# Sparse attention and token mix: scores two units ahead, exponentials in front of evictions, edge queries loaded sooner

## The chip, the cores and the metric

The kernel runs on one core of a Trainium2 chip. The metric is the device time of one execution in microseconds. The core has five engines that each work through their own queue in order: TensorE (PE: matmuls, and their weight loads PEld), VectorE (DVE), ScalarE (ACT), GpSimd (POOL) and SyncE (SP, which here only issues DMA transfers). They wait for each other by semaphores.

## The reference

Block-sparse attention over 4 batches, 8 heads, 768 positions and a head size of 64, in blocks of 32 positions (24 blocks), followed by a token mix. An inner block of queries sees its neighbours, the first and last block of keys, and three sampled blocks; the first and last block of queries see all keys.

```
scores = scale * np.matmul(q, k.transpose(0, 1, 3, 2))
mask = np.abs(blk_i - blk_j) <= window
mask = mask | (blk_i == 0) | (blk_j == 0) | (blk_i == n_blocks - 1) | (blk_j == n_blocks - 1)
...
scores = np.where(mask, scores, -1000000000.0)
attn = softmax(scores)
x = attn @ v                       # heads put side by side, d_model 512
theta = x @ w_theta
y = w_tok_r @ (x * cos(theta)) + w_tok_i @ (x * sin(theta))   # over the 768 positions
u = x + y
out = u + maximum(u @ w_ch, 0)
```

All is in float32, and the four weights of the mix come as 64-bit words that the kernel decodes into a high and a low part.

## The kernel before

The attention is cut into 56 **units**, worked on by a software pipeline that `attention` writes out by hand: under `tc.manual_schedule()` each engine runs its instructions in the order in which the Python code issues them. The units of the first two batches (bp = 0) are six edge units, named w (the first and last block of queries against a third of all keys, twice three of them), and 22 inner units (query blocks 1 to 22); then the same for the other two batches (bp = 1). `half` is 28. A unit's stages, each a function called as `do(n, stage)`:

- `scores` (L332, L340): 32 matmuls on PE (16 for an edge unit) into one of two PSUM places S, and on DVE one reduction that gives m (L343).
- `weights` (L360): four exponentials on ACT, from S and m into P.
- `turn` (L370): eight transpositions of P on PE into two PSUM banks T.
- `evict` (L376): two copies on ACT from T into pT.
- `values` (L394): matmuls of pT with the values (va, vb) on PE into X.
- `finish` (L401 to L403): the normalisation on DVE, or for an edge unit a copy (L417).

Around these run the preparations, called as `inner(n, ...)` for inner units alone. Keys of a unit are copied side by side into one of two buffers `kgs`: the window and two sampled blocks on POOL (`gather_window` L298, `gather_keys` L277), the third sampled block on ACT (`gather_key` L280). Values come by a gathering DMA that POOL issues (`gather_values` L314) and by a window load on SP, with a copy on POOL in front of it (`load_window` L310, L307). Queries come by `load_q` on SP (L242), two units at a time, and ACT scales them (`scale_q` L247). Edge queries come by `load_edges` (L258) and are scaled by `scale_edges`. `join` puts edge units together on POOL during later steps (L431). `store` writes results to a buffer in memory (L422).

Between the stages, a `Decoder` turns the weights into two parts, in shares that are due by step: ACT starts a piece (L63) and rounds its high part (L81), DVE does the rest (L68 to L86), and the raw words are loaded through ACT's queue (L59).

One step n of the loop before, as each engine sees it:

| engine | its instructions in order |
| --- | --- |
| PE | scores(n+1), turn(n), values(n-1) |
| DVE | reduction of n+1, up to two decoder shares, finish(n-1) |
| ACT | decoder start, evict(n), weights(n+1), gather_key(n+3), scale_q(n+3), decoder's high part |
| POOL | gather_window(n+3), gather_keys(n+3), gather_values(n+2), window copy of n+1, one piece of a join |
| SP | load_q(n+6), window load of n+1, store(n-1), key loads for bp = 1, edge queries at n = 24 |

After the loop comes the token mix, whose first parts `next(follow)` mixes into the last six steps. Its pools take the memory of the attention, so its bulk begins when the last unit is done. The listing has the functions around the change.

Of the kernel before, what the change touches and what calls it, by code (L numbers as in the profile page):

```python
# [10 lines left out]
F32 = mybir.dt.float32  # L11
# [8 lines left out]
P = 128  # L20
# [163 lines left out]
def attention(tc, qT, qE, kT, vr, sampled, xs, ident, early_pieces, late_pieces, first_place, follow, spares):  # L184
# [14 lines left out]
    with ExitStack() as ctx, ExitStack() as early:  # L199
# [10 lines left out]
        wp = ctx.enter_context(tc.tile_pool(name="wp", bufs=2))  # L210
# [9 lines left out]
        def make_places(bp):  # L220

            if bp == 0:
                place = first_place([P, 13824], F32, "kv0")
                k = place[:, 0:6144]
                wide[bp] = [place[:, 6144 + 1040 * c : 6144 + 1040 * (c + 1)] for c in range(6)]
            else:
                k = kp.tile([P, 6144], F32, name="k1")
                wide[bp] = vbs + vbs[:2]
            ks[bp] = k.rearrange("r (s g f) -> r s g f", s=NB, g=8)

        def load_k(bp, s0, n, queue=nc.sync):
            queue.dma_start(ks[bp][:, s0 : s0 + n].rearrange("r s g f -> r s (g f)"), kT[bp][:, s0 : s0 + n])

        def load_wide(bp, t, queue=nc.sync):
            for c in (2 * t, 2 * t + 1):
                queue.dma_start(wide[bp][c], vr[768 * bp + 128 * c : 768 * bp + 128 * c + 128])
# [16 lines left out]
        def scale_edges(bp):  # L253
            scale(qes[bp].rearrange("r b p f -> r (b p f)"))

        def load_edges(bp):
            qes[bp] = ep.tile([P, 2, 4, 64], F32, tag="qe", name=f"qe{bp}")
            nc.sync.dma_start(qes[bp].rearrange("r b p f -> r (b p f)"), qE[bp])  # L258
# [62 lines left out]
        def scores(unit):  # L321

            bp, i, x = unit
            s = st[unit] = {}
            sc = ps_s[units.index(unit) % 2].tile([P, 2, 2, 256], F32, tag="S", name=f"S{name(unit)}")
            heads = [(b, p, e) for b in range(2) for p in range(4) for e in range(2)]
            if i == "w":
                t, a = x
                q, keys = qes[bp], ks[bp][:, 8 * t : 8 * t + 8]
                for b, s_, e in [(b, p, e) for b, p, e in heads if p < 2]:  # L330
                    rows, p = slice(64 * e, 64 * e + 64), 2 * a + s_
                    nc.tensor.matmul(sc[64 * s_ : 64 * s_ + 64, e, b, :], q[rows, b, p, :], keys[rows, :, 4 * b + p, :], start=True, stop=True)  # L332
                if t == 0:
                    mxs[a] = wp.tile([P, 3, 4], F32, tag="mx", name=f"mx{name(unit)}")
                m = mxs[a][:, t]
            else:
                q, keys = qbs.pop((bp, i)), kgs[i % 2]
                for b, p, e in heads:
                    rows = slice(64 * e, 64 * e + 64)
                    nc.tensor.matmul(sc[32 * p : 32 * p + 32, e, b, :], q[rows, b, p, :], keys[rows, :, 4 * b + p, :], start=True, stop=True)  # L340
                m = wp.tile([P, 4], F32, tag="m", name=f"m{name(unit)}", bufs=2)

            nc.vector.tensor_reduce(m.rearrange("r (e b) -> r e b", e=2), sc, axis=AX.X, op=ALU.min)  # L343
            if i == "w" and t == 2:

                top = wp.tile([P, 4], F32, tag="top", name=f"top{name(unit)}", bufs=1)
                nc.vector.tensor_tensor(top, mxs[a][:, 0], mxs[a][:, 1], op=ALU.min)
                nc.vector.tensor_tensor(top, top, m, op=ALU.min)
                fs[a] = wp.tile([P, 3, 4], F32, tag="fs", name=f"fs{name(unit)}")
                nc.vector.tensor_tensor(fs[a], mxs[a], top.unsqueeze(1).to_broadcast([P, 3, 4]), op=ALU.subtract)  # L350
            s["S"] = sc, m
# [90 lines left out]
        units = []  # L442
        for bp in range(NP):
            units += [(bp, "w", (t, a)) for t in range(3) for a in range(2)] + [(bp, i, None) for i in range(1, NB - 1)]
        half = len(units) // 2

        def name(unit):
            bp, i, x = unit
            return f"{bp}_w{x[0]}{x[1]}" if i == "w" else f"{bp}_{i}"

        def do(n, stage, *args):
            if 0 <= n < len(units):
                stage(units[n], *args)

        def inner(n, stage):
            if 0 <= n < len(units) and units[n][1] != "w":
                stage(*units[n][:2])

        spares.append(lambda: qp.tile([P, 4, 4, 32], F32, tag="q", name=f"spare{len(spares)}", bufs=Q_BUFS))
        with tc.manual_schedule():
            load_edges(0)
            make_places(0)
            load_k(0, 0, 8)
            tab = Tables(nc, cp, sampled)

            nc.vector.memset(first, 0.0)
            nc.scalar.activation(first, first, AF.Exp)  # L470
            idle = ps_x.tile([P, P], F32, tag="X", name="idle")
            for _ in range(WARM):
                nc.tensor.matmul(idle, ident, ident, start=True, stop=True)
            decoder = Decoder(early_pieces + late_pieces, stage, nc.scalar)
            load_wide(0, 0)
            load_k(0, 8, 8)
            load_wide(0, 1)
            load_k(0, 16, 8)
            decoder.load(0, nc.sync)
            load_q(0, 1)  # L480
            load_wide(0, 2)
            decoder.load(1, nc.sync)
            load_q(0, 3)
            make_places(1)
            scale_edges(0)
            do(0, scores)
            making = tab.make(nc, cp)
            next(making)
            do(0, weights)
            steps = len(units) + 1  # L490
            for n in range(steps):
                if n == len(units) - 1:
                    early_s.close()
                    next(follow)

                if n <= half:
                    due = 3 * len(early_pieces) * max(n - 3, 0) // (half - 3)
                else:

                    weight = lambda k: 4 * min(k, 6) + 7 * max(k - 6, 0)  # L500
                    due = 3 * len(early_pieces) + 3 * len(late_pieces) * weight(n - half) // weight(len(units) - 4 - half)
                due = min(due, 3 * len(decoder.pieces)) - decoder.at
                decoder.first_on_scalar(due)
                do(n + 1, scores)
                next(making, None)
                inner(n + 4, number_blocks)
                inner(n + 3, gather_window)
                inner(n + 3, gather_keys)
                if due > 0:
                    decoder.on_vector()  # L510
                if due > 1 and decoder.at % 3:
                    decoder.on_vector()
                do(n, turn)
                do(n - 1, values)
                if len(units) - 2 <= n < len(units):
                    next(follow)
                do(n, evict)
                do(n + 1, weights)
                inner(n + 3, gather_key)
                inner(n + 3, scale_q)  # L520
                decoder.on_scalar()
                do(n - 1, finish)
                if units[min(n + 6, steps - 2)][:2] not in ((0, 1), (0, 3)):
                    inner(n + 6, load_q)
                inner(n + 2, gather_values)

                inner(n + 1, lambda bp, i: load_window(bp, i) if i > 2 else None)
                inner(n + 3, lambda bp, i: load_window(bp, i) if i <= 2 else None)
                inner(n - 1, store)

                if n <= len(units) and units[n - 1][1:] in (("w", (2, 0)), ("w", (2, 1))):
                    joins.append(join(units[n - 1][0], units[n - 1][2][1]))
                if n % half > 6 and joins and next(joins[0], joins) is joins:
                    joins.pop(0)
                if 5 <= n < 29 and n % 2:
                    load_k(1, n - 5, 2)
                if n == 24:
                    load_edges(1)
                if n == half - 3:
                    scale_edges(1)  # L540
                for t, step in enumerate((half - 2, half, half + 2)):
                    if n == step:
                        load_wide(1, t)

                if n == len(units) - 4:
                    early.close()
                if len(units) - 6 <= n < len(units):
                    next(follow)
            assert not decoder.left() and not joins, (decoder.left(), joins)
# [395 lines left out]
```

## Time and profile before

| what | us |
| --- | --- |
| median of three runs | 596.28 |
| lowest and highest of them | 595.65 and 603.92 |
| the profiled execution, its own time | 599.4 |
| span of its instructions | 597.6 |
| first and last reduction of an inner unit (L343) start at | 29.7 and 249.5 |

The profile shows one execution, and its times count from the first instruction. "Busy" is the time in which an engine executes an instruction. A wait is put down to the instruction whose end released it; "issue" is time in which an engine waited for nothing that the profile shows. Ends of matmuls are modelled. The granted clock is the share of full speed at which TensorE was allowed to run.

### The profile page before, as it was taken

Reading aid. Unit: us, or ns where it says so; the run is one execution under the profiler, and the core shown is the slowest. Engines: PE = TensorE matmul, PEld = TensorE weight load, DVE = VectorE, ACT = ScalarE, POOL = GpSimd, SP = SyncE. Lnnn points to the kernel's source line nnn. Section 1 sums busy time; section 2 is a strip of 40 time slices with the busy share of each in tenths; the row PEclk is TensorE's granted clock in tenths of the full one; section 3 lists DMA queues with packets and bytes.
Section 4 is the critical chain, followed back from the end, with each engine's and each line's share of the span. In section 5 each row is a group of like instructions: output and inputs, shape, how many; then the busy total and the mean of one; then the engine's idle time right before and its main releaser. Section 6 shows DMA issues by size and latency. Waiting matters only on the chain.

```text
span 597.6 us, 17323 instructions
## 1 busy us (share of the span) xinstructions
PE 548.1 (92%) x7092; PEld 436.6 (73%) x7092; DVE 423.8 (71%) x846; ACT 335.6 (56%) x684; POOL 180.8 (30%) x281
## 2 busy tenths in 40 slices
PE   6997886979967878999999999999999999999997
PEld 4765555556645545678888888888888888888886
DVE  3786876977889999968999996557732759613352
ACT  4797876758978866875565653344630445521220
POOL 1387957942687888530010010000000000000000
PEclk9898988979999998899999999999999999999999
DMA  8979889879988996852333132220212311102002
GB/s 313 353 216 263 249 254 258 233 199 318 282 242 236 238 251 184 207 159 73 94 84 104 43 89 88 89 62 10 71 36 79 95 39 34 37 27 81 1 1 105
DMA packets 53087, 86.67 MB, mean 145 GB/s; under 512 B 5392, under 2 KB 31632, under 8 KB 52624
## 3 DMA queue, kind: packets, MB, share of 16 engines
q1 hardware_dynamic: 43200, 53.28, 29.2%
q0 software_dynamic: 6944, 22.85, 14.4%
q10 hardware_dynamic: 2864, 9.44, 5.4%
q8 instruction: 56, 0.92, 0.7%
q14 instruction: 23, 0.19, 0.1%
HBM read 72.95 MB, written 12.58 MB: 143 GB/s over the span
## 4 chain that ended last, share of the span: by engine, by line
PE 36%; DVE 11%; ACT 5%; DMA 2%; issue 1%; DVEq 0%
PE ya L672 14%; PE yb L672 7%; PE o L697 2%; PE o L698 2%; PE o L699 2%; PE h L613 2%; PE h L616 2%; PE h L614 2%; ACT zh L654 2%; ACT t L623 1%; DVE rr L630 1%; DVE rr L629 1%; DVE xT L598 1%; DMA xa<-xs 1%; ACT t L622 1%
## 5 line engine op out<-in xcount | busy, mean ns | idle before, releaser
L672 PE MATMUL ya<-w_second,zh 128*128 128x512 f32 x288 | 106.9, 395 | 0.0
L672 PE MATMUL yb<-w_second,zh 128*128 128x256 f32 x288 | 80.2, 279 | 0.0
L360 ACT ACTIVATE P<-S,m 128x256 f32<-128x256 f32 x176 | 70.0, 499 | 14.9 <-DVE m L343 13.6
L370 PE MATMUL T<-ident,P 128*128 128x128 f32 x352 | 60.7, 301 | 10.0 <-ACT P L360 8.6
L370 PEld LDWEIGHTS T<-ident,P 128*128 128x128 f32 x352 | 41.7, 148 | 36.9 <-ACT P L360 29.6
L672 PEld LDWEIGHTS ya<-w_second,zh 128*128 128x128 f32 x288 | 54.1, 188 | 13.6
L343 DVE TENSOR_REDUCE m<-S 128x4 f32<-128x1024 f32 x44 | 53.6, 1217 | 10.2 <-PE S L340 9.0
L340 PE MATMUL S<-kg,q 64*32 64x256 f32 x1408 | 53.6, 390 | 7.2 <-issue 7.2
L394 PE MATMUL X<-vb,pT 128*32 128x65 f32 (+1 forms) x1408 | 50.4, 230 | 10.2 <-issue 10.1
L376 ACT COPY pT<-T 128x512 f32<-128x512 f32 x88 | 47.9, 601 | 19.4 <-PE T L370 18.9
L394 PE MATMUL X<-va,pT 128*32 128x65 f32 (+1 forms) x1408 | 50.4, 233 | 7.9 <-issue 5.4
L672 PE MATMUL ya<-w_second,zl 128*128 128x512 f32 x144 | 57.6, 400 | 0.0
L672 PEld LDWEIGHTS yb<-w_second,zh 128*128 128x128 f32 x288 | 54.3, 188 | 0.4
L314 POOL DMA_INDIRECT vb<-in_vr_dram,rows x44 | 46.1, 1047 | 20.3 <-PE X_w L394 8.6
L394 PEld LDWEIGHTS X<-va,pT 128*32 128x32 f32 (+1 forms) x1408 | 35.6, 116 | 16.7 <-issue 12.4
L394 PEld LDWEIGHTS X<-vb,pT 128*32 128x32 f32 (+1 forms) x1408 | 37.9, 117 | 12.2 <-issue 12.0
L705 DVE SCALAR_TENSOR_TENSOR of<-o,xT 128x512 f32<-128x512 f32 (+1 forms) x24 | 13.3, 557 | 46.0 <-PE o L699 42.5
L672 PE MATMUL yb<-w_second,zl 128*128 128x256 f32 x144 | 40.6, 282 | 0.0
L307 POOL COPY va<-va 32x1040 f32<-32x1040 f32 (+1 forms) x28 | 31.6, 1129 | 27.8 <-DMA va<-in_vr_dram 20.9
L613 PE MATMUL h<-w_theta_hi,xh 128*128 128x512 f32 x96 | 38.2, 398 | 0.4 <-ACT xh L602 0.4
L340 PEld LDWEIGHTS S<-kg,q 64*32 64x32 f32 x1408 | 23.0, 107 | 20.5 <-issue 11.7
L614 PE MATMUL h<-w_theta_lo,xh 128*128 128x512 f32 x96 | 37.9, 394 | 0.0
(169 smaller groups left out, 1309.2 us busy)
## 6 DMA issues: line engine op xcount, KB each, us to landing
va<-in_vr_dram SPq DMA_DIRECT2D x58, 130.0 KB
q<-in_qT_dram SPq DMA_DIRECT2D x22, 256.0 KB
xs<-xo SPq DMA_DIRECT2D x22, 256.0 KB
xr<-xs SPq DMA_DIRECT2D x22, 256.0 KB
xa<-xs SPq DMA_DIRECT2D x88, 64.0 KB
raw_tok_r<-in_w_tok_r_dram ACTq DMA_DIRECT2D x8, 576.0 KB
out_dram<-of SPq DMA_DIRECT2D x16, 256.0 KB
kv<-in_vr_dram SPq DMA_DIRECT2D x6, 520.0 KB
```

What stands on the lines that cost most here:

```text
L307: nc.gpsimd.tensor_copy(va[rows], vas[(i + 1) % 2][rows])
L314: nc.gpsimd.indirect_dma_start(out=vbs[(i + 1) % VB][rows], out_offset=None, in_=vr, in_offset=bass.IndirectOffsetOnAxis(ap=tab.rows[rows, ...
L340: nc.tensor.matmul(sc[32 * p : 32 * p + 32, e, b, :], q[rows, b, p, :], keys[rows, :, 4 * b + p, :], start=True, stop=True)
L343: nc.vector.tensor_reduce(m.rearrange("r (e b) -> r e b", e=2), sc, axis=AX.X, op=ALU.min)
L360: nc.scalar.activation(pt[:, e, b], sc[:, e, b], AF.Exp, bias=m[:, 2 * e + b : 2 * e + b + 1], scale=-1.0)
L370: nc.tensor.transpose(banks[k // 4][:, k % 4], pt[:, (k // 2) % 2, k % 2, 128 * (k // 4) : 128 * (k // 4) + 128], ident)
L376: nc.scalar.copy(out[:, 4 * h : 4 * h + 4], bank)
L394: nc.tensor.matmul(s["X"][rr, b, e, :], s["T"][0:rows, 4 * c + 2 * e + b, rr], v[0:rows, v0 : v0 + 65], start=c == 0, stop=c == 1,)
L613: nc.tensor.matmul(ps, hi[:, c, :], wh[:, c, :], start=c == 0, stop=False)
L614: nc.tensor.matmul(ps, hi[:, c, :], wl[:, c, :], start=False, stop=False)
L672: nc.tensor.matmul(acc, z[:, dd], wt[:, t0 : t0 + n], start=first and (n == 512 or c % 2 == 0), stop=last, skip_group_check=n == 256,)
L705: nc.vector.scalar_tensor_tensor(o, ps, 0.0, xT[b][:, e : e + groups, t0 : t0 + n], op0=ALU.max, op1=ALU.add)
```

## The change

In the loop, `scores` moves from n+1, ahead of everything, to n+2, right behind `turn(n)`; `turn(n)` itself moves up to the place where scores stood. A call for unit 1 is put in front of the loop, and m gets a third buffer. `weights(n+1)` stands ahead of `evict(n)`. `scale_q` and `load_q` move one unit ahead. The edge queries of bp = 1 are loaded at step 18 and scaled at step half - 4.

```
-                m = wp.tile([P, 4], F32, tag="m", name=f"m{name(unit)}", bufs=2)
+                m = wp.tile([P, 4], F32, tag="m", name=f"m{name(unit)}", bufs=3)
...
             do(0, weights)
+            do(1, scores)
...
                 decoder.first_on_scalar(due)
-                do(n + 1, scores)
+                do(n, turn)
+                do(n + 2, scores)
                 next(making, None)
                 inner(n + 4, number_blocks)
                 inner(n + 3, gather_window)
...
-                do(n, turn)
                 do(n - 1, values)
                 if len(units) - 2 <= n < len(units):
                     next(follow)
+                do(n + 1, weights)
                 do(n, evict)
-                do(n + 1, weights)
                 inner(n + 3, gather_key)
-                inner(n + 3, scale_q)
+                inner(n + 4, scale_q)
                 decoder.on_scalar()
                 do(n - 1, finish)
-                if units[min(n + 6, steps - 2)][:2] not in ((0, 1), (0, 3)):
-                    inner(n + 6, load_q)
+                if units[min(n + 7, steps - 2)][:2] not in ((0, 1), (0, 3)):
+                    inner(n + 7, load_q)
                 inner(n + 2, gather_values)
...
-                if n == 24:
+                if n == 18:
                     load_edges(1)
-                if n == half - 3:
+                if n == half - 4:
                     scale_edges(1)
```

## The prediction

> **What bounds the kernel now.** I read the page first, then the busy table by stage, then the waits of each stage, then the timeline around the longest of them.
>
> ```profile
> PE 548.1 (92%) x7092; PEld 436.6 (73%) x7092; DVE 423.8 (71%) x846; ACT 335.6 (56%) x684; POOL 180.8 (30%) x281
> q8 instruction: 56, 0.92, 0.7%
> ```
>
> From 262 us on, PE is full with the token mix, which the diff does not touch; the change can only act on the 56 attention units before it. The table below (columns: stretch, length, then PE, PEld, DVE, ACT, POOL busy us with instruction counts, granted TensorE clock, DMA share, GB/s) cuts them into the first half's inner units, the edge units, two parts of the second half, and the tail.
>
> ```profile
> 29.70:123.20 93.50, 77.66 (x2127) 53.98 (x2127) 74.65 (x136) 73.21 (x173) 74.83 (x110) 0.95 0.86 243
> 123.20:156.20 33.00, 28.97 (x572) 20.34 (x571) 25.37 (x46) 25.35 (x60) 9.84 (x18) 0.90 0.93 266
> 156.20:205.00 48.80, 38.31 (x1115) 26.61 (x1116) 44.38 (x74) 40.14 (x93) 41.03 (x61) 1.00 0.90 255
> 205.00:249.40 44.40, 35.86 (x938) 24.01 (x936) 43.02 (x75) 31.84 (x75) 33.11 (x46) 0.92 0.85 216
> 249.40:262.00 12.60, 12.14 (x235) 9.69 (x236) 9.49 (x26) 11.23 (x22) 5.17 (x8) 1.00 0.53 135
> ```
>
> No engine is full in the first stretch. In the fourth, DVE is busy 43.02 of 44.40 us: there its work is the bound. For the others the waits decide (engine line, what it waited for, us in total, times, longest). First stretch:
>
> ```profile
> DVE sm L401 <- PE X L394: 8.9, 6, 3.6
> DVE m L343 <- PE S L340: 7.1, 10, 2.1
> PE X L394 <- issue: 9.6, 6, 3.1
> PE S L340 <- issue: 2.7, 2, 2.5
> PE T L370 <- ACT P L360: 1.3, 2, 0.9
> ```
>
> DVE waits for PE, and PE waits for "issue", which is no engine and no tile. The timeline puts these gaps inside a run of matmuls whose operands are ready, and the busy table between three neighbouring gaps of the second half has the same count each time:
>
> ```profile
> 60.63 0.63 PE L340 MATMUL S<-kg,q 64*32 64x256 f32 x6 [2.49 <-issue]
> 167.07:173.16 6.09, 4.17 (x126) 2.79 (x125) 5.69 (x9) 4.91 (x12) 4.50 (x7) 1.00 0.76 230
> 173.17:178.28 5.11, 4.15 (x126) 2.72 (x126) 4.70 (x11) 4.13 (x9) 4.93 (x8) 1.00 0.89 244
> 178.29:184.58 6.29, 4.99 (x125) 3.46 (x126) 5.53 (x9) 5.04 (x14) 5.56 (x9) 1.00 0.89 233
> ```
>
> Some 252 PE instructions lie between gaps, and the page's instruction queue moved 56 packets for 2 x 7092 PE instructions: 253 a packet, 16 KB each. So I read the gaps as PE waiting for its next block of code, which travels on DMA engines that are 0.76 to 0.93 busy here. The gaps fall wherever the block ends, whatever the order of the program.
>
> The Trainium skill, "Runtime: NRT & Kernel Launch", section "Instruction fetch mechanics", says that code comes in 16 KiB blocks of 256 instructions, the next one fetched while the current one runs, and that crossing a boundary is mostly hidden. The size agrees with the 253 above; "hidden" does not agree with the 2.49 us gap. By that rule these gaps would be something that another order can remove, which is the first rival below.
>
> **The change, part by part.**
>
> (1) *Scores two units ahead, behind the transposition.* No matmul, reduction or exponential is added. PE's order goes from S(n+1), T(n), X(n-1) to T(n), S(n+2), X(n-1). A free-running unit shows PE's own pace:
>
> ```profile
> 63.25 1.09 PE L340 MATMUL S<-kg,q 64*32 64x256 f32 x32
> 64.28 1.09 PE L370 MATMUL T<-ident,P 128*128 128x128 f32 x8
> 66.34 1.09 PE L340 MATMUL S<-kg,q 64*32 64x256 f32 x32
> L343 DVE TENSOR_REDUCE m<-S 128x4 f32<-128x1024 f32 x44 | 53.6, 1217 | 10.2 <-PE S L340 9.0
> L360 ACT ACTIVATE P<-S,m 128x256 f32<-128x256 f32 x176 | 70.0, 499 | 14.9 <-DVE m L343 13.6
> L376 ACT COPY pT<-T 128x512 f32<-128x512 f32 x88 | 47.9, 601 | 19.4 <-PE T L370 18.9
> ```
>
> From S to S is 66.34 - 63.25 = 3.09 us, against 93.5 us for the 21 units whose reductions start in the first stretch, or 4.45 each. Before, T(n+1) waits within one step for a reduction of 1.22 us, the eviction (47.9/44 = 1.09) and the exponentials (70.0/44 = 1.59); after, that chain has a step more. ACT's 13.6 us of waiting for m and 18.9 for T shrink, but only what PE or DVE gets back shortens the stage. In the first stretch PE is busy 77.66 and waits 9.6 + 2.7 = 12.3 on issue, together 89.96. If the code gaps stay, 93.50 - 89.96 = 3.5 us is all that the order can save, the lower bound being nothing. About half goes, since the end of the stretch has DVE as full as the fourth: **-1.9**.
>
> (2) *Third stretch.*
>
> ```profile
> PE X L394 <- issue: 5.0, 5, 1.7
> PE S L340 <- issue: 4.5, 3, 1.9
> ```
>
> PE 38.31 + 5.0 + 4.5 = 47.81 of 48.80: at most 1.0 to save, **-0.7**. *Fourth stretch:*
>
> ```profile
> PE T L370 <- ACT P L360: 7.1, 5, 2.2
> ```
>
> Here the very wait that the new order removes is largest, 7.1 us. But the exponentials are late because DVE is full; with 43.02 of 44.40 busy and the rest small gaps, what is late next is DVE's own queue. Bounds 0 and -1.4; **0**. *Tail:* PE is busy 12.14 of 12.60, since the token mix's first matmuls stand between the last units; bounds 0 and -0.5, **0**.
>
> (3) *Edge queries loaded at step 18, not 24, and scaled a step sooner.*
>
> ```profile
> 120.83 0.42 SPq L258 DMA_DIRECT2D qe<-in_qE_dram  x1
> 126.98 0.63 ACT L247 ACTIVATE qe<-qe 128x512 f32<-128x512 f32 x1 [4.32 <-DMA qe<-in_qE_dram]
> DVE da_tok_r L68 <- ACT da_tok_r L63: 3.9, 1, 3.9
> PE S_w L332 <- ACT qe L247: 2.8, 1, 2.8
> 128.00:134.80 6.80, 6.54 (x100) 4.15 (x96) 6.30 (x12) 5.88 (x14) 2.46 (x3) 0.50 0.71 191
> ```
>
> ACT stands 4.32 us for a transfer issued 6.2 us earlier; behind it, in ACT's own queue, are the decoder's start (DVE waits 3.9 for it), an eviction and four exponentials. PE waits 2.8, then runs 6.8 us at a granted clock of 0.50. Six steps earlier is some 6 x 4.45 = 27 us: the wait goes whole. The load passes six steps of SP's issues at 0.42 us each way. Gain: at least PE's 2.8; at most 2.8 plus half of 6.54, 6.1; I take DVE's wait, which lies between: **-3.9**. Late next is the code block or DVE.
>
> (4) *Exponentials before evictions.* Evictions now queue on ACT behind exponentials that need m(n+1). m(n+1) is a step old by then, so this costs **0**; the cover is that step. Uncovered, X(n) would be up to 1.59 late in a unit. What it gains is part of the shorter waits in (1), with the same bounds.
>
> (5) *q loaded at n+7 and scaled at n+4, for a scores call one step sooner.* The distance stays three steps, and the slot's last reader has moved as well; the third m buffer costs nothing. On SP the load passes one step's issues; SP idles anyway:
>
> ```profile
> 67.98 1.38 SPq L242 DMA_DIRECT2D q<-in_qT_dram  x1
> SPq L310 <- PE X L394: 100.0, 35, 9.9
> ```
>
> **0**, at worst 1.38 us on a window load that has a step's time.
>
> (6) *The new wait.* POOL still gathers keys three units ahead, but S now wants them a step sooner, right behind T, and X(n-1) is queued behind S on PE; DVE's normalisation waits for X. Two samples, a free one and one while POOL also joins edge units (POOL's last gather, then the T behind which S would stand):
>
> ```profile
> 65.42 0.74 POOL L277 COPY kg<-kv 128x256 f32 x2
> 67.37 1.41 PE L370 MATMUL T<-ident,P 128*128 128x128 f32 x8
> 113.79 1.49 POOL L277 COPY kg<-kv 128x256 f32 x2
> 113.29 1.86 PE L370 MATMUL T<-ident,P 128*128 128x128 f32 x8 [0.93 <-ACT P L360]
> ```
>
> Margins: 68.78 - 66.16 = 2.6 us, and 115.15 - 115.28 = -0.1. T itself comes up to one S (1.09) sooner. So it costs 0 to some 4 x 1.2 = 4.8 us over the last four units before the edges; DVE is full there, so near the low end: **+0.5**. *Prologue:* one S more in front of the loop, nothing less overall, +/-1.1, **0**.
>
> The sum is -1.9 - 0.7 - 3.9 + 0.5 = -6.0 us. It reaches the end whole, as the token mix starts on the last X:
>
> ```profile
> 261.08 1.14 POOL L59 DMA_DIRECT2D raw_tok_i<-in_w_tok_i_dram  x2 [5.57 <-PE X L394]
> ```
>
> The profiled execution took 599.4 us (span 597.6), 3.1 above the median 596.28. It would become 593.4; on the median, **590.3 us**.
>
> **The rivals.** *A: the gaps go too.* If DVE, with a unit more in hand, no longer feels PE's gaps, its waits 8.9 + 7.1 + 3.9 = 19.9 us go: 576.4. For it: DVE is only 74.65 of 93.50 busy in the first stretch. Against it: PE's 89.96 there. It decides if the gaps shrink by half (6 us, so 584). The skill's rule leads to the same place, since hidden fetches would leave PE nothing but waits on other engines. *B: only the edge load counts.* PE's block times eat whatever the order frees, because a block that PE finishes sooner waits longer for the next: -3.9 + 0.5, so 592.9; nothing in the profile speaks against it but the 3.5 us. *C: slower.* The gather becomes the bound as in (6). Every unit would have to look like the second sample. The 6.0 us gained and 2% (11.9 us) are used up at 17.9/44 = 0.41 us of lateness a unit; at one S per unit (1.09) it is 44 x 1.09 - 6 = 42 us slower, 638. The free sample's 2.6 us speaks against it. *D: nothing at all*, 596: the edge load still late; a lead of six steps excludes that nearly.
>
> **How the numbers follow.** Forecast 50%, A 20%, B 20%, C 5%, D 5%. The likeliest gives 590.3. Its own range runs from every gain at its bound (-3.5 - 1.0 - 1.4 - 0.5 - 6.1 - 1.1 = -13.6, so 582.7) to the smallest ones with the full new wait (-2.8 + 4.8 = +2.0, so 598.3). A changed rhythm of transfers can also move the code gaps, a few tenths on each of some 35 blocks, either way. The stated range, 581 to 598, is that one, let down a little towards A: half of A and all of B and D lie inside. More than 2% faster means below 584.4: 18%, mostly A. More than 2% slower, over 608.2: 5%, C. Within 2%, about what a measurement of this kernel can tell from no change: 77%.
>
> **What the changed profile would show.** Right: ACT's wait for qe and PE's 2.8 us are gone and no clock of 0.50 follows them; T's waits for P and ACT's for m shrink; PE's issue waits stay near 12.3 us in the first and 9.5 in the third stretch, still every 250 instructions; DVE stays over 95% busy in the last 45 us. Wrong: issue waits fall by half (A), S waits for POOL's gathers in most units (C), or DVE's busy time itself changes.

## The result, and the profile after

The changed kernel is slower: 619.35 us median of four runs (611.43 to 620.71) against 600.1 (595.65 to 609.61) for the kernel before in the same series, a ratio of 1.0294 with a 95% interval of 1.0217 to 1.0371. The forecast was 590.3, the range ended at 598. Ratios here and below leave disturbed runs out on both sides, so they are not quite the quotients of the medians.

The profiled execution took 619.56 us, its span is 617.8, 20.2 more than before. All of it was lost in the attention: the 44 reductions of inner units (L343) run from 27.4 to 268.4 us, 241.0 us, where they took 249.5 - 29.7 = 219.8. The first fence has the busy line of the page after, and four of its groups (busy us, mean ns of one, then idle time in front of them and what ended most of it).

```profile
PE 547.3 (89%) x7092; PEld 438.8 (71%) x7092; DVE 435.0 (70%) x846; ACT 333.0 (54%) x684; POOL 181.8 (29%) x281
...
L370 PE MATMUL T<-ident,P 128*128 128x128 f32 x352 | 57.3, 314 | 36.8 <-ACT pT L376 34.6
...
L343 DVE TENSOR_REDUCE m<-S 128x4 f32<-128x1024 f32 x44 | 53.6, 1219 | 32.9 <-PE S L340 32.8
...
L360 ACT ACTIVATE P<-S,m 128x256 f32<-128x256 f32 x176 | 69.2, 486 | 1.7 <-DVE m L343 1.7
...
L376 ACT COPY pT<-T 128x512 f32<-128x512 f32 x88 | 48.5, 625 | 0.0
```

Every engine executes as many instructions as before. PE's busy time is 547.3 against 548.1, and ACT's exponentials and copies take what they took. DVE's is 435.0 against 423.8: instructions of the decoder's lines (L68 to L86) took longer, and only those. That alone does not make the loss, since the last kernel but one below (shares first, edge queries late) has 435.2 and is no slower than the kernel before (ratio 0.9991). What the change was meant to shorten did get shorter: ACT's wait for m fell from 13.6 to 1.7 us, and its wait for T from 18.9 to nothing. Two waits took their place, T for the eviction and the reduction for S. The table of waits says where they begin. First the kernel before, over its whole attention from 29.7 to 249.4 us (us in total, times, longest), ACT, PE and DVE in turn:

```profile
ACT pT L376 <- PE T L370: 18.9, 16, 4.0
ACT P L360 <- DVE m L343: 13.6, 13, 2.8
ACT da_tok_r L63 <- DVE sm L402: 2.6, 3, 1.2
PE X L394 <- issue: 15.5, 12, 3.1
PE S L340 <- issue: 7.2, 5, 2.5
DVE m L343 <- PE S L340: 9.0, 14, 2.1
```

The same for the changed kernel, from 29.7 to 262 us (its last inner reduction starts at 268.4; up to there T's wait for pT comes to the 34.6 us of the page):

```profile
ACT da_tok_r L63 <- DVE sm L402: 18.5, 4, 6.7
ACT w_second L81 <- DVE da_tok_i L70: 12.8, 5, 4.1
...
PE T L370 <- ACT pT L376: 30.7, 17, 4.3
PE X L394 <- issue: 11.2, 8, 3.2
PE S L340 <- issue: 6.2, 5, 2.8
DVE m L343 <- PE S L340: 31.1, 19, 3.5
DVE sm L401 <- PE X L394: 0.2, 1, 0.2
```

ACT now stands at the decoder's instructions, L63 (start of a piece) and L81 (its high part). In the kernel before these waits were 2.6 us and a few small ones. They wait for DVE, DVE's reduction waits for PE, PE's T waits for ACT: a ring. One turn of it can be followed in the chain of waits of the changed kernel in order of time (start us, us, what; short pieces are left out but for the raw load):

```profile
51.82 1.14 PE T L370 x8
52.96 1.11 PE S L340 x32
...
54.16 1.23 DVE m L343
55.39 0.61 DVE da_theta L85
...
56.02 0.69 DVE w_theta_lo L86
...
57.01 0.07 ACTq L59
...
57.13 0.30 ACT da_theta L63
...
58.05 1.20 ACT P L360 x3
59.25 0.96 ACT pT L376 x2
60.21 0.31 ACT kg L280
60.52 0.67 issue
61.20 1.97 PE T L370 x8
```

Read downwards: T(n), then S(n+2), which now stands behind it on PE; the reduction of n+2; the decoder's low part (L85, L86), which stands behind that reduction on DVE; the next raw load on ACT's queue (L59), which overwrites words that L86 reads; the start of a piece (L63), behind the load; exponentials; the eviction behind them; and T(n+2), which needs the bank that the eviction of n+1 empties. The 0.98 us between that eviction and T(n+2) are a copy of ACT (L280) and 0.67 us of issue. From T to T 61.20 - 51.82 = 9.38 us for two units, where the kernel before needed 2 x 4.45 = 8.9. This turn loses only half a microsecond; over the first 20 units the changed kernel takes 97.16 us, 4.86 a unit, against 90.12, 4.51 a unit. Nothing in the ring can overlap anything else in it, so whatever delays one member delays all. One such delay is PE's own: the granted clock was 1.00 from 51.8 to 54.1 us, where T and S take 2.3 us, and 0.55 from 61.2 to 65.0, where the next T and S take 3.8. How much of the loss comes by this was not tried by itself. The timeline around 98 us shows the ring with a gap of PE (in brackets the idle time in front, and what ended it):

```profile
97.91 0.64 PE L340 MATMUL S<-kg,q 64*32 64x256 f32 x9 [2.82 <-issue]
...
98.68 1.22 DVE L343 TENSOR_REDUCE m<-S 128x4 f32<-128x1024 f32 x1 [3.51 <-PE S L340]
...
100.61 2.63 DVE L86 TENSOR_TENSOR w_first<-da_tok_r,raw_tok_r 128x576 fp32r<-128x576 f32 x1
...
103.27 0.33 ACTq L59 DMA_DIRECT2D raw_tok_r<-in_w_tok_r_dram  x1
...
103.65 0.72 ACT L63 ACTIVATE da_tok_r<-raw_tok_r 128x576 f32<-128x576 f32 x1 [6.69 <-DVE sm L402]
```

A code gap of 2.82 us within S becomes 3.51 us of the reduction's wait, then L86 is slow, and ACT has stood 6.69 us when the raw load at last goes out at 103.27, just after L86 has ended at 103.24. The table of waits calls this "da_tok_r L63 <- DVE sm L402", the event nearest in time; the order of the queue names the load behind L86.

### The profile page after: what moved, and what is told of

Same layout as the page of the kernel before. It is cut to its first block, busy times and chain, and to the rows that moved or that the text cites. A ratio compares the mean times of both kernels' runs of the same rounds, so it can differ in the third digit from the quotient of the medians.

```text
span 617.8 us, 17360 instructions
## 1 busy us (share of the span) xinstructions
PE 547.3 (89%) x7092; PEld 438.8 (71%) x7092; DVE 435.0 (70%) x846; ACT 333.0 (54%) x684; POOL 181.8 (29%) x281
## 4 chain that ended last, share of the span: by engine, by line
PE 71%; DVE 12%; ACT 7%; issue 4%; DMA 4%; SPq 1%; ACTq 0%; DVEq 0%
PE ya L674 22%; PE yb L674 11%; PE S L340 6%; PE T L370 5%; ACT P L360 3%; PE h L615 3%; PE h L618 3%; PE h L616 3%; DVE m L343 3%; PE o L699 3%; PE o L700 3%; PE o L701 3%; PE X L394 2%; ACT pT L376 2%; PE T_w L370 2%
## 5 line engine op out<-in xcount | busy, mean ns | idle before, releaser
L370 PE MATMUL T<-ident,P 128*128 128x128 f32 x352 | 57.3, 314 | 36.8 <-ACT pT L376 34.6
L343 DVE TENSOR_REDUCE m<-S 128x4 f32<-128x1024 f32 x44 | 53.6, 1219 | 32.9 <-PE S L340 32.8
L370 PEld LDWEIGHTS T<-ident,P 128*128 128x128 f32 x352 | 44.2, 158 | 44.0 <-ACT pT L376 38.7
L340 PE MATMUL S<-kg,q 64*32 64x256 f32 x1408 | 58.5, 430 | 6.2 <-issue 6.2
L674 PEld LDWEIGHTS ya<-w_second,zh 128*128 128x128 f32 x288 | 54.1, 188 | 13.6
L394 PE MATMUL X<-va,pT 128*32 128x65 f32 (+1 forms) x1408 | 48.8, 233 | 6.2 <-issue 5.2
L394 PE MATMUL X<-vb,pT 128*32 128x65 f32 (+1 forms) x1408 | 48.0, 229 | 6.1 <-issue 6.1
L394 PEld LDWEIGHTS X<-va,pT 128*32 128x32 f32 (+1 forms) x1408 | 34.3, 116 | 26.0 <-issue 16.3
L340 PEld LDWEIGHTS S<-kg,q 64*32 64x32 f32 x1408 | 23.9, 116 | 25.6 <-issue 20.0
L394 PEld LDWEIGHTS X<-vb,pT 128*32 128x32 f32 (+1 forms) x1408 | 36.2, 117 | 7.5 <-issue 7.5
```

Source lines behind the costliest of these rows:

```text
L370: nc.tensor.transpose(banks[k // 4][:, k % 4], pt[:, (k // 2) % 2, k % 2, 128 * (k // 4) : 128 * (k // 4) + 128], ident)
L394: nc.tensor.matmul(s["X"][rr, b, e, :], s["T"][0:rows, 4 * c + 2 * e + b, rr], v[0:rows, v0 : v0 + 65], start=c == 0, stop=c == 1,)
L674: nc.tensor.matmul(acc, z[:, dd], wt[:, t0 : t0 + n], start=first and (n == 512 or c % 2 == 0), stop=last, skip_group_check=n == 256,)
```

## The experiments

Theory M: the ring as above. It closes over two orders, DVE's (reduction ahead of the decoder's shares) and ACT's (decoder instructions ahead of exponentials and eviction). Other explanations at hand were that the exponentials in front hold T's banks too long (theory B below), that S two ahead meets POOL's gathers, and that the code gaps grew; the last is settled by the tables above, where the issue waits of X and S fell from 22.7 to 17.4 us. The first eight kernels ran in two series of four (the kernel before 604.1 and 601.6 us); medians are given with the ratio to the kernel before in the same series.

**Edge queries sooner, alone**, in the kernel before:

```
-                if n == 24:
+                if n == 18:
...
-                if n == half - 3:
+                if n == half - 4:
```

> The kernel before with the edge queries alone moved (loaded at step 18, scaled at step 24). The prediction's term: 3.9 us faster than the kernel before, and ACT's wait of 4.3 us for qe gone. Rival: the freed time is eaten by PE's code gaps or by DVE, less than 1 us.

Measured: 600.93 us, ratio 0.9993 (0.9932 to 1.0053). ACT's wait of 4.3 us for qe is gone from the trace, but the gain is too small to be seen; 3.9 us would be 0.9935, just inside the interval.

**The shares first**: the changed kernel with DVE's decoder shares ahead of the reduction.

```
                 decoder.first_on_scalar(due)
+                if due > 0:
+                    decoder.on_vector()
+                if due > 1 and decoder.at % 3:
+                    decoder.on_vector()
                 do(n, turn)
...
                 inner(n + 3, gather_keys)
-                if due > 0:
-                    decoder.on_vector()
-                if due > 1 and decoder.at % 3:
-                    decoder.on_vector()
```

> The changed kernel with DVE's decoder shares in front of the reduction of unit n+2. Theory M (a loop over two steps: share - ACT's raw load, start or high part - exponentials - eviction - T - S - reduction - next share): the shares no longer wait for PE, ACT's waits for DVE's shares (about 39 us in the changed kernel's attention) fall below 15 us, T's 34.6 us for pT below 15, and the time falls to 585 to 602. Theory B (the exponentials in front of the evictions hold T's two banks too long): nothing of this loop matters, the time stays at 611 to 621.

Measured: 596.13 us (594.27 to 603.25), ratio 0.993 (0.9879 to 0.9981). With four lines in another place, the loss of 2.9% is gone, and a gain of 0.7% stands in its place. Its waits from 29.7 to 262 us, as above:

```profile
ACT w_first L81 <- DVE da_tok_r L70: 3.8, 3, 1.9
...
PE T L370 <- ACT pT L376: 14.3, 13, 2.3
PE S L340 <- POOL kg L277: 7.4, 11, 1.1
...
DVE m L343 <- PE S L340: 6.3, 7, 2.5
```

ACT's decoder waits are small again, the reduction's wait falls from 31.1 to 6.3 and T's from 30.7 to 14.3. This is what theory M says of opening the ring on DVE. Three more kernels with the shares first follow below, and the loss is gone in each of them (0.9979, 0.9951, 0.9991).

**Scores in front of the transposition**, still two ahead: `do(n + 2, scores)` and `do(n, turn)` change places in the changed kernel.

> The changed kernel with S(n+2) in front of T(n) on PE. Theory M: T and the eviction leave the loop (about 2.2 of 9.4 us over two steps), T may still wait for pT but the reduction no longer does, DVE's 32.6 us of waiting for S falls by more than half, and the time falls to 592 to 608. Theory B: T's wait for its banks is PE's bound and stays, since X is still behind it; 611 to 621.

Measured: 607.58 us, ratio 1.0112 (1.0004 to 1.022). S no longer stands behind T, and T's wait for evictions is gone, but S now comes before its keys are gathered, as the waits of PE in this kernel show:

```profile
PE S L340 <- issue: 21.2, 14, 4.7
PE S L340 <- POOL kg L277: 17.5, 12, 4.9
```

So a part of the loss goes with this edge of the ring too; by the middle value it is more than half, but the interval leaves that open. The reduction's wait for S falls from 31.1 to 19.8 us, less than by the half that was expected. What remains shows as the gather, the prediction's third rival, and as issue waits.

**The eviction first**: `do(n, evict)` ahead of `do(n + 1, weights)` in the changed kernel, as before the change.

> The changed kernel with the eviction in front of the exponentials again, scores still two ahead behind T. Theory B: the loss goes, 590 to 602, and T's 34.6 us for pT fall below 10. Theory M: the loop closes through the exponentials of P instead, T waits for P where it waited for pT, 606 to 621.

Measured: 619.86 us, ratio 1.0355 (1.0224 to 1.0485): no better. PE's T then waits for P (25.2 us in 14 waits) where it waited for pT. Which of the two stands first behind the decoder's instructions makes no difference that can be seen, and the rival that the exponentials hold the banks falls.

**Raw loads on SP**: `Decoder(early_pieces + late_pieces, stage, nc.sync)` in the changed kernel, for `nc.scalar`.

> The changed kernel with the decoder's raw words loaded through SP's queue instead of ACT's, so that ACT no longer stands at a load until DVE's low part is done. Theory M: ACT's waits of the decoder's start for DVE (25.7 us in the changed kernel, with 8.2 us more shown as issue) go, those of the high parts stay; 600 to 612. If the load is not part of the loop: 614 to 621.

Measured: 619.78 us, ratio 1.0277 (1.0195 to 1.0359), where theory M expected 600 to 612: the loss stays whole. The waits at L63 are gone, and in the table of waits of this kernel those at the high part L81, which waits for the bits (L70) of a share, have grown from 23.9 to 60.9 us over four rows, of which the first and the last:

```profile
ACT w_second L81 <- DVE da_tok_i L70: 16.9, 5, 5.0
...
ACT w_first L81 <- DVE da_tok_r L70: 13.9, 4, 4.9
```

So the ring has two closings on ACT side by side, and taking one away leaves the other.

**The high part a step later**: exponentials and then `decoder.on_scalar()` moved up right behind `first_on_scalar`, so that a high part stands behind one more unit's exponentials.

```
                 decoder.first_on_scalar(due)
+                do(n + 1, weights)
+                decoder.on_scalar()
                 do(n, turn)
...
-                do(n + 1, weights)
                 do(n, evict)
...
-                decoder.on_scalar()
```

> The changed kernel with ACT's high parts a step later, behind that step's exponentials, so that ACT no longer stands at them until DVE's bits are done. Theory M: ACT's waits of the high parts for DVE (23.9 us) go, those at the loads stay; 600 to 613. If they are not part of the loop: 614 to 621.

Measured: 613.69 us, ratio 1.0197 (1.0127 to 1.0267), between the two expectations. A third of the loss goes by the middle value; this time the waits at L63 stay (11.0 + 10.6 + 7.7 + 3.9 + 3.5 us).

**Both of these together:**

> Both of the two edits above, with DVE's order left as in the changed kernel. Theory M: the loop is open, T's wait for pT falls below 15 us and the time reaches that of the shares in front of the reduction, 588 to 602. Rival: DVE's order itself costs (the reduction waits for S while a share could run), so that 605 or more remains.

Measured: 605.58 us, ratio 1.0079 (1.0037 to 1.0122). With both closings opened, most of the loss is gone, by a way that leaves DVE's order alone, and T's wait for pT is below 15 us as expected. But the time misses the 588 to 602 of theory M, and the rival's 605 or more came. What remains is probably that order itself: the reduction still waits for S with the shares queued behind it, as the waits of this kernel show:

```profile
ACT P L360 <- DVE m L343: 28.8, 25, 3.2
...
PE T L370 <- ACT pT L376: 13.9, 7, 3.4
...
DVE m L343 <- PE S L340: 20.9, 17, 2.9
```

**Exponentials first, alone**, in the kernel before: `do(n + 1, weights)` ahead of `do(n, evict)`.

> The kernel before with the exponentials in front of the eviction alone, scores one unit ahead in front of T. Prediction's term: 0. Theory M agrees within 1%: no share stands behind a reduction that waits for T. Rival: the eviction waits for m(n+1), which here belongs to the same step, and X behind it; slower by more than 1%.

Measured: 603.58 us, ratio 1.0055 (1.0013 to 1.0096). With scores one ahead, m is not old: ACT waits 43.9 us for it in 31 places, T 24.0 us for the eviction, and still the whole costs half a per cent. The order on ACT alone is not where 2.9% went.

The last four ran in a third series (the kernel before 601.65).

**Shares and eviction first**: the shares-first kernel with `evict` ahead of `weights`.

> The changed kernel with the decoder's shares ahead of the reduction and the eviction ahead of the exponentials, so with neither of the two orders that closed the loop. With the shares first alone, exponentials waited 16.7 us on ACT and T waited 14.3 for evictions behind them. Theory M (a loop over DVE's and ACT's queues): an eviction that passes the waiting exponentials takes away most of T's 14.3 us, some of it comes back at the code gaps: 590 to 595. Rival (once the loop is open, ACT's order no longer matters, because PE is bound by its code gaps and POOL's gathers): 595 to 598, with T's wait replaced by waits of S for kg.

Measured: 601.45 us, ratio 0.9979 (0.9939 to 1.002). The rest of T's wait for pT goes (1.5 us), but both expectations are missed, the 590 to 595 of theory M and the rival's 595 to 598: ACT now waits 21.2 us for T, and T itself for P and for code.

**The same with raw loads on SP:**

> As the run with shares and evictions first, and the decoder's raw loads issued by SP, so that ACT no longer waits for a DMA issue. Theory M: with the loop open nothing stands behind the loads on ACT any more, so no change against that run, within 0.3%. Rival (the raw loads on ACT's queue cost by themselves): 3 to 5 us faster than that run.

Measured: 599.01 us, ratio 0.9951 (0.9917 to 0.9985), no difference to the run above that the intervals could tell. Once the ring is open, ACT's order and its loads hardly matter.

**Shares first, edge queries late**: the shares-first kernel with steps 24 and half - 3.

> The kernel with the shares first (596.1 against 600.1), with the edge queries loaded and scaled as before (steps 24 and half - 3). If the gain of that kernel is the edge queries' (the prediction's -3.9, hidden in the spread when they were moved alone), this one falls back to the kernel before: 600 to 602, ratio 0.997 to 1.0. If the gain is that of the scores two ahead without the loop, and the edges bring nothing, it stays at 0.991 to 0.995.

Measured: 601.53 us, ratio 0.9991 (0.9958 to 1.0024). ACT's wait for qe is back (5.2 us) and with it PE's at the edge scores (4.5 us). Against 0.993 with the edges sooner that is 0.6%, 3.7 us, but the two come from different series and their intervals overlap. It leans to the first reading, that this kernel's gain is the edge queries'; against that, the run with shares and eviction first has the edges sooner and 0.9979 in the same series.

**Shares first in the kernel before**, nothing else changed.

> The kernel before with nothing but the decoder's shares moved ahead of the reduction. Theory M: in the kernel before no loop runs over the shares, since S stands in front of T on PE; moving the shares only makes the reduction some 1.2 to 2.5 us later in steps with shares, and T waits for exponentials behind it: 600 to 606, ratio 1.0 to 1.01. Rival (the gain of the kernel with shares first is that of DVE's order alone, whatever PE's order): 0.990 to 0.995.

Measured: 636.56 us, ratio 1.0565 (1.0501 to 1.063). Both expectations miss. The move that mends the changed kernel costs the kernel before 5.7%. Its timeline of ACT:

```profile
53.32 0.47 ACT L360 ACTIVATE P<-S,m 128x256 f32<-128x256 f32 x1 [0.42 <-DVE sm L401]
...
55.05 0.70 ACT L63 ACTIVATE da_theta<-raw_theta 128x512 f32<-128x512 f32 x1
...
59.80 1.57 ACT L360 ACTIVATE P<-S,m 128x256 f32<-128x256 f32 x4 [3.08 <-DVE sm L401]
```

And of DVE, in the same stretch:

```profile
55.79 0.89 DVE L68 TENSOR_SCALAR da_theta<-da_theta 128x512 f32<-128x512 f32 x1 [1.83 <-ACT da_theta L63]
...
57.60 0.98 DVE L70 SCALAR_TENSOR_TENSOR da_theta<-raw_theta,da_theta 128x512 int32<-128x512 int32 x1
58.50 1.21 DVE L343 TENSOR_REDUCE m<-S 128x4 f32<-128x1024 f32 x1
```

The timelines show another ring, over one step: exponentials of n, the start of a piece behind them on ACT, its share on DVE, the reduction of n+1 behind the share, the exponentials of n+1. From 53.32 to 59.80 it takes 6.5 us for one unit, and ACT's exponentials wait 56.5 us for DVE from 29.7 to 262 us. With scores one ahead, the exponentials of this step need the reduction of this step, so the reduction must go first; with scores two ahead they need that of the step before, and the shares may. This second ring is read from the timelines; no run opened it.

## Why the prediction was wrong

**Part (1), -1.9, bounded by nothing and -3.5: the step that failed.** Right that no work is added, that m would be older and that ACT's waits for m and T would shrink. Wrong that S(n+2) behind T(n) could cost nothing at worst: the kernel lost 20.2 us of span. The bound came from PE's busy time and waits in the trace of before, and such a sum can say what an order may gain, not what it may lose. The step "after, that chain has a step more" followed only one unit's own chain, from reduction over exponentials and eviction to T. It did not ask what else stands in the two queues that this chain crosses: on DVE the decoder's shares behind a reduction that now waits for T, and on ACT the load, start and high part ahead of the exponentials. The runs showed that wait in place of a gain: the reduction waits 31.1 us for S where it waited 9.0, and T 30.7 for evictions. The shares-first kernel and the kernel with both closings opened show the ring as the cause of most of it from its two sides, each without touching the other. The gain of this part was not seen even with the ring open: with the shares first and the edge queries late, which leaves the other parts, the ratio is 0.9991 (0.9958 to 1.0024), too wide to exclude the 1.9 us.

**Part (4), 0, "the cover is that step".** It held for m: exponentials wait 1.7 us for it. This order is a member of the ring but not the fault: with the eviction first again the loss stays (619.86 us), T waiting for P in place of pT, and alone in the kernel before it costs half a per cent.

**Part (2), -0.7 and 0.** The later stages lost as well. By the start of the 21st reduction (119.85 before, 124.54 after, measured from the first one at 29.73 and 27.38) 7.0 us of the 21.2 were gone; the other 14.2 came behind it.

**Part (3), -3.9.** The mechanism was right: the wait for qe is gone wherever the load is at step 18. The size stays open. Alone it gave 0.9993 (-0.4 us, with nearly 4 us of uncertainty on either side), under the shares-first order some 3.7 us between two series.

**Part (5), 0.** No wait for q appears that would speak against it; the one row that names a DMA of q (part of the ring's chain) stands at a raw load. It was not tried alone.

**Part (6), +0.5.** In the changed kernel S never waits long for POOL's gathers, since the ring makes PE late. In the open ring it does, 7.4 us in eleven waits, more than the upper bound of 4.8; much of it is likely hidden, since that kernel is no slower than the kernel before. This part did ask who stands behind S, and stopped at PE's own queue (X and the normalisation); that wait fell from 8.9 to 0.2 us. DVE's queue behind the reduction is what it left out.

**The rivals.** A falls: the issue waits of X and S together went from 22.7 to 17.4 us, a quarter and not half, and between the four gaps from 97.9 to 117.4 us there are still 252 to 254 PE instructions each time. B and D, a smaller gain and none, are excluded by the sign. C had the right sign and the wrong place; its wait was seen at any length only where the ring was opened (17.5 us with S in front of T). The 5% for slower was too little for a change that moves a wait past two in-order queues.

**The signs.** One sign of being wrong came that the prediction had named: DVE's busy time changed, by 11.2 us. Why the decoder's instructions ran longer stays open; what the traces show of it is in the last section. DVE was to stay over 95% busy in the last 45 us, and is busy 39.8 of the 45.4 us up to the last reduction.

## What to carry to other kernels

Where an operation is moved behind another on one engine, follow not only its own chain but, on each engine that the chain crosses, whatever stands behind the waiting instruction, side work and DMA issues included, until the path ends or comes back; a path that comes back is a ring, and its length divided by the units in one turn (9.4 / 2 = 4.7 here) must stay below the time of a unit (4.45 here). The place of side work belongs to the lookahead: the same four lines in front of the reduction took away a loss of 2.9% with scores two ahead and brought one of 5.7% with scores one ahead. If taking one wait away lets another grow and the time stays, as with the raw loads on SP, look for a second way round the same ring.

## What the runs showed of the hardware

An instruction of DVE can take several times as long beside a row of POOL's operations. In the shares-first kernel, DVE's timeline has the same instruction twice:

```profile
58.02 3.16 DVE L76 TENSOR_SCALAR ds_theta<-da_theta 128x512 int32<-128x512 int32 x1
...
71.57 0.41 DVE L76 TENSOR_SCALAR ds_theta<-da_theta 128x512 int32<-128x512 int32 x1
```

POOL's timeline beside the first of them:

```profile
57.91 1.07 POOL L307 COPY va<-va 64x1040 f32<-64x1040 f32 x1
58.93 0.74 POOL L431 TENSOR_TENSOR xw_w<-xw_w 128x260 f32<-128x260 f32 x1
59.61 0.61 POOL L298 COPY kg<-kv 128x512 f32<-128x512 f32 x1
60.16 0.73 POOL L277 COPY kg<-kv 128x256 f32 x2
```

It took 0.41 us at 71.57 and 3.16 us at 58.02, ending at 61.18, when the last of POOL's five operations in a row had ended at 60.16 + 0.73 = 60.89. The slow L86 of 2.63 us in the changed kernel also ran beside a row of POOL's copies. The Trainium skill, "SBUF — State Buffer", section "Who interferes with whom", says that DVE shares a pair of ports with POOL, that an instruction with two inputs in this memory (as L86 has) contends with POOL's reads through it, and that in DVE's two-port modes, which `tensor_scalar` can enter, whichever engine issues first holds the pair for its whole instruction while the other is blocked. These rows agree, with the addition that here DVE's instruction outlasted several of POOL's. That L76 ran in such a mode, and that the ports are the reason, was not tried by itself. In a ring this matters, since nothing covers it.
